# Smaller first loads, and another engine for the store, in a streaming attention and FFN decode step

## Chip, cores and metric

The kernel runs on one core of a Trainium2 chip. The metric is device time in microseconds (us) for one execution, and of several executions the median. A profiled execution gives, beside its own time, a span: from the first to the last instruction that the profiler recorded. The engines are TensorE (PE, with PEld for its weight loads), VectorE (DVE), ScalarE (ACT), GpSimd (POOL) and SyncE (SP). SP does no arithmetic here; it issues the transfers (DMAs) and waits. The name SPq or ACTq in a profile line is the queue of that engine's instructions which wait or issue.

## What is computed

One decode step for a batch of 8 with one new token each (x is 8 x 512). Branch A is attention over the last 1024 entries of a cache of 4096; branch B is a gated feed-forward network. All inputs are bf16.

```python
xn = _layernorm(x)                                  # 8 x 1 x 512
# A: 32 query heads, 8 K/V heads, head size 128, window W = 1024
q = (xn @ wq).reshape(B, Sq, Hq, Dh).transpose(0, 2, 1, 3)
k = jnp.repeat(k_cache[:, :, Sk - W:, :], rep, axis=1)
v = jnp.repeat(v_cache[:, :, Sk - W:, :], rep, axis=1)
p = _softmax(jnp.einsum("bhqd,bhkd->bhqk", q, k) * (Dh ** -0.5))
s = o_merged(jnp.einsum("bhqk,bhkd->bhqd", p, v)) @ wo
# B
g = _silu((_gelu(xn @ w_gate) * (xn @ w_up)) @ w_down)
return x + s * g
```

(`o_merged` stands for the transpose and reshape that join the heads.) The input of 47.46 MB is read once: 16 MiB of K, 16 MiB of V, 4 MiB of wq, 4 MiB of wo, 5.25 MiB of the feed-forward weights. The output is 8 KB.

## The kernel before

**Buffers.** Eight slots of 2 MiB each (128 partitions x 16 KB) in one ring hold everything large: a batch's K or V, half of wq, a weight matrix of the feed-forward part, or half of wo. A slot is loaded again once its last readers are done.

**Loads.** `load_cache` (L69) loads one batch's K or V: two transfers (g = 0 and 1, four heads each) of 1 MiB, L72. Partition p*4 + n of the destination holds 32 consecutive rows of head n, 8 KB in one piece. All loads are issued by SP, in the order of the program text: K of batch 0, wq in two transfers of 2 MiB (L93: partition p gets four rows of wq of 8 KB each, two to a transfer, so 16 KB in one piece), K of batch 1, V of batch 0; then in the loop over batches (L398 on) K of batch b+2 and V of batch b+1; at the end w_gate, w_up, w_down (L422, L425) and wo in six transfers (L436), of which the last three are of 640, 256 and 128 KB, so that little is left to do after the last one has landed. The load of x (L67) is the only transfer that ACT issues.

**Landing semaphores.** Each transfer tells of its landing by a semaphore. There are eight of them for the transfers, given out in rotation in the order of the program text, whichever engine issues: x has the first, the first K transfer the second, and so on. An issue waits until the transfer eight before it has landed, as that one has the same semaphore. The store of the output is the 45th transfer. At the end of the program SP waits for all semaphores, one after the other (the profile puts these waits at L538), then for the other engines.

**Compute.** The layer norm of x and its transposed copy xnR come first. VectorE turns K (`turn_k`, L234, one instruction for a transfer's 1 MiB, so both halves of the partitions have to be there), TensorE computes q in 32 matmuls (L247, eight for each quarter k of wq), which go through `q_both` (L257, L260) to `qbd` (L269). Then for each batch: scores (L295), softmax (L305 to L317), the turned probabilities (L328), values (L339), and the collection of heads (L360 to L391). The feed-forward part runs after the last batch (L450 to L491). Last come the 128 matmuls with wo (L498), 32 for each of its four quarters, then y (L506), out_sb (L508) and the store (L510).

**Order.** The schedule is by hand: each engine runs its instructions in the order of the program text, and waits only for what they need.

Of the kernel before, what the change touches and what calls it, by code (L numbers as in the profile page):

```python
# [21 lines left out]
def kernel(  # L22
# [13 lines left out]
    nc = tc.nc  # L36

    B, Sq, D = A_x.shape
    Hkv, Sk, Dh = A_k_cache.shape[1], A_k_cache.shape[2], A_k_cache.shape[3]
# [3 lines left out]
    win0 = Sk - W  # L43
    F = B_w_gate.shape[1]
    inv = float(Dh) ** -0.5
    P = nc.NUM_PARTITIONS
    NK = D // P
    HG = 4
    NG = Hkv // HG
    C = W * HG // P  # L50
# [11 lines left out]
    def slot(name):  # L62
        return ring.tile([P, 2 * ROW], BF16, name=name, tag="slot")
# [2 lines left out]
    x_sb = keep.tile([B, D], BF16, name="x_sb")  # L66
    nc.scalar.dma_start(out=x_sb, in_=A_x.flatten_outer_dims())  # L67

    def load_cache(cache, b, name):  # L69
        t = slot(name).rearrange("p (g x) -> p g x", g=NG)  # L70
        for g in range(NG):
            nc.sync.dma_start(  # L72
                out=t[:, g],
                in_=cache[b, g * HG : (g + 1) * HG, win0:Sk, :].rearrange(
                    "n (p c) d -> p n (c d)", c=C
                ),
            )
        return t

    k_sb, v_sb = {}, {}  # L80

    def load_k(b):
        k_sb[b] = load_cache(A_k_cache, b, "k_sb")

    def load_v(b):
        v_sb[b] = load_cache(A_v_cache, b, "v_sb")

    load_k(0)
    wq_v = A_wq.rearrange("(p k) n -> p k n", k=NK)
    wq_sb = []  # L90
    for i in range(2):
        t = slot("wq_sb").rearrange("p (k n) -> p k n", k=NK // 2)
        nc.sync.dma_start(out=t, in_=wq_v[:, i * (NK // 2) : (i + 1) * (NK // 2), :])  # L93
        wq_sb += [t[:, k, :] for k in range(NK // 2)]
    load_k(1)
    load_v(0)

# [4 lines left out]
        out=ident,  # L102
        in_=ident,
# [13 lines left out]
        out=xpad,  # L117
        in_=xpad,
# [17 lines left out]
        out=xhat,  # L136
# [9 lines left out]
    with tc.tile_pool(name="ps_x", bufs=1, space=PSUM) as ps_x:  # L146
# [26 lines left out]
        out=hv,  # L173
        in_=hv,
# [7 lines left out]
        out=neg_st,  # L182
        in_=neg_st,
# [8 lines left out]
        out=neg_mv,  # L192
        in_=neg_mv,
# [12 lines left out]
    for g in range(NG):  # L206
        nc.vector.tensor_reduce(
            out=sel[:, g, g * qd : (g + 1) * qd],
            in_=ident.rearrange("p (t g h) -> p g h t", t=4, g=NG)[:, g],
# [5 lines left out]
        out=own, in_=ident.rearrange("p (i e) -> p e i", e=8), axis=AX.X, op=ALU.add  # L215
    )
    pick = consts.tile([P, 4 * NU], BF16, name="pick")
    with nc.allow_low_precision(reason="sums of zeros and a single one"):
        nc.vector.tensor_reduce(
            out=pick, in_=ident.rearrange("p (a e) -> p a e", e=8), axis=AX.X, op=ALU.add  # L220
# [177 lines left out]
    for b in range(B):  # L398
        if b + 2 < B:
            load_k(b + 2)  # L400
        if b + 1 < B:
            load_v(b + 1)
            turn_k(b + 1, 0)
        softmax(b)
        if b + 1 < B:
            scores(b + 1, 0)
        if b >= 1:
            gather(b - 1)
        if b + 1 < B:
            turn_k(b + 1, 1)  # L410
            scores(b + 1, 1)
        turn_p(b)
        values(b)
        keep_o(b)
        if b == 4:
            regroup(0)
# [10 lines left out]
    for u in range(NU):  # L427
        if u % 2 == 0:
            pair = slot("wo_sb").rearrange("p (v j d) -> p v j d", v=2, d=D)
        t = pair[:, u % 2]  # L430
        src = A_wo[u * 1024 : (u + 1) * 1024, :].rearrange("(p j) d -> p j d", j=8)
# [14 lines left out]
    for n, ws in (("z_ps", wgu[0]), ("u_ps", wgu[1])):  # L446
# [15 lines left out]
        out=z2, in0=z2, scalar1=0.044715, scalar2=1.0, op0=ALU.mult, op1=ALU.add  # L462
# [11 lines left out]
        out=hT.rearrange("p j b -> p (j b)"), in_=h_bf.rearrange("p (y j) -> p j y", j=NJ)  # L474
    )
    f_ps = ps_f.tile([P, DT], FP32, name="f_ps")
    for j in range(NJ):
# [11 lines left out]
        out=g_sb, in0=g_sb, scalar1=0.5, scalar2=0.5, op0=ALU.mult, op1=ALU.add  # L489
# [5 lines left out]
    for u in range(NU):  # L495
# [11 lines left out]
    out_sb = ffn.tile([P, DT], BF16, name="out_sb")  # L507
    nc.vector.tensor_tensor(out=out_sb, in0=y, in1=x_res, op=ALU.add)  # L508
    out_f = out.flatten_outer_dims()
    nc.sync.dma_start(  # L510
        out=out_f.rearrange("b (t d) -> t b d", t=4), in_=out_sb[0 : P : RB, :]
    )

# [29 lines left out]
```

## Time and profile before

| What | Value |
|---|---|
| median of three runs | 121.58 us (121.34 to 121.73) |
| profiled execution, own time | 121.8 us |
| its span | 119.7 us |
| busy: PE, DVE, ACT | 74.1, 75.8, 31.4 us |
| moved | 47.61 MB, mean 398 GB/s over the span |
| packets on the queue of the transfers that SP issues | 6228 |
| packets on the queue of the transfer that ACT issues (x) | 16 |
| mean granted TensorE clock | 0.837 |

The page divides the span into 40 equal slices; a digit is the busy share in tenths, and the DMA row is the mean over the core's 16 DMA engines. A row of a group of instructions says the line, the engine, what is written and read, the number and the time. A row of transfers says who issues them, how many, the KB of each, and the median time from issue to landing; that time includes the wait behind the transfers issued earlier. A transfer consists of packets, and the trace has a record of each: its start, its length in ns and its bytes; every DMA engine that takes part in a transfer ends it with a small write of 4 bytes to the semaphore.

The shortest and longest times from issue to landing of the K and V transfers are 5.4 and 24.4 us. The issuing instruction itself takes 535 ns in the middle of the run and up to 662 ns at its start.

### The profile page before, as it was taken

The numbers are of one execution on the slowest core, as the hardware profiler recorded it, in microseconds if no ns is written. First come the engines' busy times: TensorE is split into PE (matmuls) and PEld (weight loads), VectorE is DVE, ScalarE is ACT, GpSimd is POOL, SyncE is SP. The second block draws the span as 40 slices with busy tenths as digits, with TensorE's granted clock in tenths as the row PEclk, the third lists the DMA queues.
The fourth block names the chain that finished last, engine by engine and source line by source line (L and its number), as shares of the span: only waits on it lengthen the run. The fifth ranks groups of instructions, "written<-read, shape, count | busy, mean of one in ns | idle before, by whom it ended". The sixth has DMA issues, their size and how long they took to land.

```text
span 119.7 us, 2300 instructions
## 1 busy us (share of the span) xinstructions
PE 74.1 (62%) x992; PEld 38.7 (32%) x992; DVE 75.8 (63%) x101; ACT 31.4 (26%) x75; POOL 3.2 (3%) x10
## 2 busy tenths in 40 slices
PE   0100499811994988969687684992994547535460
PEld 0100133300341544535443351450353433134340
DVE  3698820499739999999859959909943232651010
ACT  4600000676007151441612510700616110200000
POOL 2150000000000000000000000000000000000000
PEclk9999999985599999999999998599589755555555
DMA  2999999999999999999999999999999999999930
GB/s 66 394 457 433 411 416 427 430 433 422 427 427 433 419 419 427 435 411 430 430 433 405 430 430 430 411 430 435 424 419 447 422 451 412 434 403 430 402 118 3
DMA packets 6254, 47.61 MB, mean 398 GB/s; under 512 B 732, under 2 KB 868, under 8 KB 1124
## 3 DMA queue, kind: packets, MB, share of 16 engines
q1 hardware_dynamic: 6228, 47.46, 94.5%
q8 instruction: 8, 0.13, 0.4%
q10 hardware_dynamic: 16, 0.01, 0.0%
q14 instruction: 2, 0.02, 0.0%
HBM read 47.46 MB, written 0.01 MB: 397 GB/s over the span
## 4 chain that ended last, share of the span: by engine, by line
DMA 63%; PE 16%; DVE 14%; issue 2%; ACT 2%; SPq 1%; DVEq 0%
DMA wo_sb<-in_A_wo_dram 20%; DMA k_sb<-in_A_k_cache_dram 17%; DMA v_sb<-in_A_v_cache_dram 16%; DMA wq_sb<-in_A_wq_dram 9%; PE q_ps L247 8%; PE S_ps L295 6%; DVE kT L234 5%; DVE qbd L269 2%; DVE mx L305 2%; DVE q_both L260 1%; ACT P_sb L317 1%; PE s_ps L498 1%; DVE q_both L257 1%; SPq L72 1%; PE O_ps L339 1%
## 5 line engine op out<-in xcount | busy, mean ns | idle before, releaser
L295 PE MATMUL S_ps<-kT,qbd 128*128 128x512 bf16 x128 | 34.4, 416 | 14.9 <-DVE kT L234 11.5
L234 DVE STREAM_TRANSPOSE kT<-k_sb 128x2048 int32<-128x2048 int32 x16 | 36.5, 2289 | 4.6 <-DMA k_sb<-in_A_k_cache_dram 4.6
L295 PEld LDWEIGHTS <-qbd 128*128 128x128 bf16 x128 | 12.9, 103 | 32.4 <-issue 17.0
L247 PE MATMUL q_ps<-wq_sb,xnR 128*128 128x512 bf16 x32 | 9.8, 482 | 8.8 <-DMA wq_sb<-in_A_wq_dram 8.8
L315 ACT ACTIVATE nb<-m 32x1 f32<-32x1 f32 x32 | 6.4, 201 | 22.7 <-DVE m L312 22.4
L305 DVE TENSOR_REDUCE mx<-S_ps 128x1 f32<-128x1024 f32 x8 | 9.6, 1195 | 4.1 <-PE S_ps L295 4.1
L317 ACT ACTIVATE P_sb<-S_ps,nb 128x1024 bf16<-128x1024 f32 x8 | 11.1, 1391 | 0.3
L339 PE MATMUL O_ps<-v_sb,pT 128*32 128x128 bf16 x512 | 9.3, 228 | 2.6 <-DVE pT L328 2.6
L339 PEld LDWEIGHTS <-pT 128*32 128x32 bf16 x512 | 7.8, 101 | 5.6 <-issue 3.0
L352 ACT COPY O_sb<-O_ps 128x256 f32<-128x256 f32 x8 | 3.0, 372 | 23.5 <-PE O_ps L339 23.5
L247 PEld LDWEIGHTS <-xnR 128*128 128x128 bf16 x32 | 3.7, 118 | 14.6 <-issue 12.6
L328 DVE STREAM_TRANSPOSE pT<-P_sb 128x512 int32<-128x512 int32 x8 | 5.7, 711 | 3.4 <-ACT P_sb L317 2.8
L257 ACT CAST q_both<-q_ps 128x512 bf16<-128x512 f32 x6 | 3.0, 613 | 16.7 <-PE q_ps L247 16.7
L360 PE MATMUL o_ps<-O_sb,sel 128*32 128x128 f32 x32 | 6.1, 325 | 0.9 <-ACT O_sb L352 0.9
L498 PE MATMUL s_ps<-wo_sb,oT 128*32 128x128 bf16 x128 | 4.4, 307 | 3.4 <-DMA wo_sb<-in_A_wo_dram 3.3
L284 PE MATMUL S_ps<-neg_mv,neg_st 128*128 128x512 bf16 x16 | 4.8, 381 | 1.9 <-DVE q_both L257 1.9
L257 DVE CAST q_both<-q_ps 128x512 bf16<-128x512 f32 x2 | 1.3, 672 | 6.9 <-ACT q_both L257 6.9
L360 PEld LDWEIGHTS o_ps<-O_sb,sel 128*32 128x32 f32 x32 | 3.4, 128 | 5.0 <-issue 1.7
L498 PEld LDWEIGHTS <-oT 128*32 128x32 bf16 x128 | 3.5, 136 | 4.4 <-issue 4.2
L506 DVE TENSOR_TENSOR y<-s_ps,g_sb 128x128 f32<-128x128 f32 x1 | 0.3, 290 | 6.9 <-PE s_ps L498 6.9
L239 DVE MEMSET qbd<- 128x4096 uint32 x1 | 3.5, 3472 | 0.8 <-issue 0.8
L479 PE MATMUL f_ps<-wd_sb,hT 128*32 128x128 bf16 x56 | 1.7, 311 | 3.2 <-DVE hT L473 3.2
(64 smaller groups left out, 48.9 us busy)
## 6 DMA issues: line engine op xcount, KB each, us to landing
k_sb<-in_A_k_cache_dram SPq DMA_DIRECT2D x16, 1024.0 KB, 19.9
v_sb<-in_A_v_cache_dram SPq DMA_DIRECT2D x16, 1024.0 KB, 19.6
wq_sb<-in_A_wq_dram SPq DMA_DIRECT2D x2, 2048.0 KB, 11.3
wo_sb<-in_A_wo_dram SPq DMA_DIRECT2D x3, 1024.0 KB, 25.0
wgu_sb<-in_B_w_gate_dram SPq DMA_DIRECT2D x1, 1792.0 KB, 21.3
wgu_sb<-in_B_w_up_dram SPq DMA_DIRECT2D x1, 1792.0 KB
wd_sb<-in_B_w_down_dram SPq DMA_DIRECT2D x1, 1792.0 KB, 24.9
wo_sb<-in_A_wo_dram SPq DMA_DIRECT2D x1, 640.0 KB, 24.1
```

The lines of the kernel that those rows point to most:

```text
L234: nc.vector.transpose(out=t.bitcast(I32), in_=k_sb[b][:, g].bitcast(I32))
L247: nc.tensor.matmul(q_ps[i], xnR[:, k, :, :].rearrange("p j b -> p (j b)"), wq_sb[k][:, i * 512 : (i + 1) * 512], start=(k == 0), stop=(k = ...
L257: e(out=q_bf[:, i * 512 : (i + 1) * 512], in_=q_ps[i])
L284: nc.tensor.matmul(S[b][:, half, :], neg_st.rearrange("p j h -> p (j h)"), neg_mv.rearrange("p a n -> p (a n)"), start=True, stop=False,)
L295: nc.tensor.matmul(S[b][:, half, :], qbd[:, m, b, w, g, :], kv[:, half * 16 : (half + 1) * 16, m, :, w], start=False, stop=(g == NG - 1 an ...
L305: nc.vector.tensor_reduce(out=mx, in_=S[b].rearrange("p a c -> p (a c)"), axis=AX.X, op=ALU.max)
L315: nc.scalar.mul(nb[32 * j : 32 * j + 32, :], m1, -inv)
L317: nc.scalar.activation(out=P_sb[b].rearrange("p c i w -> p c w i"), in_=S[b].rearrange("p a (c w i) -> p (a c) w i", w=2, i=32), func=ACT.Exp,
L328: nc.vector.transpose(out=pT[b].rearrange("p c h w -> p (c h w)").bitcast(I32), in_=P_sb[b].rearrange("p c i w -> p (c i w)").bitcast(I32),)
L339: nc.tensor.matmul(O_ps[b][32 * t : 32 * t + 32, g, :], pT[b][:, c // 2, :, c % 2], vv[:, c, :], start=(c < 4), stop=(c >= C - 4),)
L360: nc.tensor.matmul(o[:, 0:Dh], sel[:, g, :], O_sb[b][:, g, :], start=(g == 0), stop=(g == NG - 1))
L498: nc.tensor.matmul(s_ps[32 * t : 32 * t + 32, :], oT[:, j, u, :], wo[u][:, j, t * DT : (t + 1) * DT], start=(u == 0 and j == 0), stop=(u = ...
```

## The change

Three things. The first transfer of K (batch 0, g = 0) is issued as two, for partitions 0 to 63 and for partitions 64 to 127. wq is loaded by four transfers of 1 MiB, one for each quarter k, into the same two slots. The store of the output is issued by ACT instead of SP. There are 48 transfers now, and the store is the 48th, so that it has the last of the eight semaphores.

```diff
-    def load_cache(cache, b, name):
+    def load_cache(cache, b, name, parts=None):
         t = slot(name).rearrange("p (g x) -> p g x", g=NG)
         for g in range(NG):
-            nc.sync.dma_start(
-                out=t[:, g],
-                in_=cache[b, g * HG : (g + 1) * HG, win0:Sk, :].rearrange(
-                    "n (p c) d -> p n (c d)", c=C
-                ),
+            src = cache[b, g * HG : (g + 1) * HG, win0:Sk, :].rearrange(
+                "n (p c) d -> p n (c d)", c=C
             )
+            if parts is not None and g == 0:
+                parts(t[:, g], src)
+            else:
+                nc.sync.dma_start(out=t[:, g], in_=src)
         return t
...
+    def first_load(dst, src):
+        for a, z in ((0, P // 2), (P // 2, P)):
+            nc.sync.dma_start(out=dst[a:z], in_=src[a // HG : z // HG])
+
     def load_k(b):
-        k_sb[b] = load_cache(A_k_cache, b, "k_sb")
+        k_sb[b] = load_cache(A_k_cache, b, "k_sb", first_load if b == 0 else None)
...
         t = slot("wq_sb").rearrange("p (k n) -> p k n", k=NK // 2)
-        nc.sync.dma_start(out=t, in_=wq_v[:, i * (NK // 2) : (i + 1) * (NK // 2), :])
-        wq_sb += [t[:, k, :] for k in range(NK // 2)]
+        for k in range(NK // 2):
+            nc.sync.dma_start(out=t[:, k, :], in_=wq_v[:, i * (NK // 2) + k, :])
+            wq_sb.append(t[:, k, :])
...
-    nc.sync.dma_start(
+    nc.scalar.dma_start(
         out=out_f.rearrange("b (t d) -> t b d", t=4), in_=out_sb[0 : P : RB, :]
     )
```

## The prediction

> **What bounds the kernel now.** I read the slices of the span first, then the same by stages, then the issues of transfers, and last the end of the span instruction by instruction.
>
> ```profile
> PE   0100499811994988969687684992994547535460
> DVE  3698820499739999999859959909943232651010
> DMA  2999999999999999999999999999999999999930
> GB/s 66 394 457 433 411 416 427 430 433 422 427 427 433 419 419 427 435 411 430 430 433 405 430 430 430 411 430 435 424 419 447 422 451 412 434 403 430 402 118 3
> ```
>
> Each column is a fortieth of 119.7 us, 2.99 us. TensorE and VectorE both have holes; the DMA row has none from the second column to the thirty-eighth, and the rate stays near 427 GB/s. By stages (start:end, length, busy us of PE, PEld, DVE, ACT, POOL, clock, DMA share, GB/s):
>
> ```profile
> 0.00:3.00 3.00, 0.00 (x0) 0.00 (x0) 0.98 (x4) 1.28 (x1) 0.78 (x7) 1.00 0.29 66
> 8.00:13.00 5.00, 0.00 (x0) 0.00 (x0) 4.19 (x3) 0.00 (x0) 0.00 (x0) 1.00 1.01 433
> 40.00:60.00 20.00, 17.21 (x271) 9.43 (x269) 19.02 (x18) 7.84 (x21) 0.00 (x0) 1.00 1.01 426
> 100.00:112.00 12.00, 6.79 (x152) 4.16 (x145) 4.33 (x9) 1.40 (x3) 0.00 (x0) 0.50 1.01 425
> 112.00:116.00 4.00, 2.17 (x64) 1.69 (x63) 0.00 (x0) 0.00 (x0) 0.00 (x0) 0.50 0.63 250
> ```
>
> The DMA share is 1.01 from 8 to 112 us: one stream, never starved. So the time is the stream's start, its bytes, and a tail. The chain of waits names many buffers and engines on its way, but where a transfer takes 20 us from issue to landing it stood behind others, and an engine that is 1 us sooner doesn't move it.
>
> ```profile
> k_sb<-in_A_k_cache_dram SPq DMA_DIRECT2D x16, 1024.0 KB, 19.9
> wq_sb<-in_A_wq_dram SPq DMA_DIRECT2D x2, 2048.0 KB, 11.3
> ...
> x_sb<-in_A_x_dram ACTq DMA_DIRECT2D x1, 8.0 KB
> ```
>
> The end, and SP's longest waits there:
>
> ```profile
> 114.87 1.28 PE L498 MATMUL s_ps<-wo_sb,oT 128*32 128x128 bf16 x32 [0.46 <-DMA wo_sb<-in_A_wo_dram]
> 116.20 0.29 DVE L506 TENSOR_TENSOR y<-s_ps,g_sb 128x128 f32<-128x128 f32 x1 [6.91 <-PE s_ps L498]
> 116.52 0.29 DVE L508 TENSOR_TENSOR out_sb<-y,x_res 128x128 bf16<-128x128 f32 x1
> 116.84 0.69 SPq L510 DMA_DIRECT2D out_dram<-out_sb  x1
> ```
> ```profile
> SPq L510 <- DVE out_sb L508: 15.1, 1, 15.1
> SPq L538 <- DMA out_dram<-out_sb: 1.0, 1, 1.0
> ```
>
> The last matmuls wait for the last wo piece (landed at 115.81 by its semaphore's record); behind them come two VectorE instructions, 0.69 us of issue, 1.0 us of landing, and SP's final waits up to 119.7.
>
> The profiled execution took 121.8 us (span 119.7, and 2.1 around it), the median of the three runs is 121.58; the sum below is a difference, laid on the median.
>
> **The change part by part.**
>
> *First K transfer in two halves.* Removed: one transfer of 1 MiB to 128 partitions. Added: two of 0.5 MiB to partitions 0 to 63 and 64 to 127, one behind the other. At the head of the stream the first half has its 64 partitions to itself. No large transfer of this trace goes to fewer than 128 partitions, so the price has two ends. The only narrow load is x, 8 KB to 8 partitions. By its packet records seven of its eight 1 KB packets took 44 to 51 ns, the same as the 46 ns of wo's 1 KB packets on 128 partitions; by these a narrow transfer loses nothing: 0. But as a whole, from its first packet (1.753 us) to its last end (2.060), x took 0.307 us: 8,192 B / 0.307 us = 26.7 GB/s for 8 partitions, and 427 x 8/128 is 26.7 too. If the rate goes with the partitions, 64 get 213.5 GB/s: 524,288 B take 2.46 us, both halves 4.91, against 2.46 for 1 MiB at 427: +2.45 us. The engines don't start together (first K packets spread over 0.28 us, about 0.1 between two); where two share what one had, an engine that is 0.1 ahead wins that twice: -0.2. I take **+2.25**: a half MiB is nearer to a whole transfer than to a 44 ns packet, which a buffer on the way could swallow. Ends 0 and +2.45. Nothing covers it: each transfer behind starts that much later, SP's waits for landings pass later, and the stream has no idle time in which to catch up. Late next is the first K transpose (7.08 us), then wq, then everything.
>
> The Trainium skill, "SBUF — State Buffer", section "Door 1: The DMA port swizzle", says that partitions 0 to 63 reach only 8 of the 16 ports on the DMA side and gives 196 GB/s for 64 partitions against 328 for 128 (1 MiB each); the section on issuing two DMAs for both halves says they serialize. By its limit of 218 GB/s the halves would cost an estimated +2.4 us, by the packets' 44 ns row nothing: the page speaks against this part, and no transfer here shows it at size.
>
> *The earlier start.* x's first packet came 0.37 us after its issue ended (8 packets), K's 0.78 us after (128 packets): 0.41 for 120 more packets. With 64 fewer: -0.22 if it goes by packets, 0 if it is fixed. I take **-0.15**, as K's sixteen first packets come one after the other over 0.28 us, which looks like a making by number.
>
> *wq in four.* Two transfers of 2 MiB become four of 1 MiB. Packets of 16 KB (256 of them) become 8 KB; on one engine they follow each other every 607 ns and 307 ns: 2 x 307 - 607 = 7 ns for each of 16 packets an engine, 0.11 us. Three more transfers than before, K's included, put three more completion writes on each engine, 9 ns and about 6 between: 0.05. Together **+0.16**, ends 0.05 and 0.16. The gain: the first q matmul can start after 1 MiB, some 2.4 us before 13.6; but the last needs the same last byte, and q's consumers feed compute that waits for the stream: **0**, hidden behind the DMA row. Three more issues on SP, some 0.58 us each (the opening eight took 0.48 to 0.66): 1.74 us. What hides them is the queue: before the first landing SP has issued at least 7 MB of which under 2 have moved, 12 us of stream. Without that cover, 0.58 each.
>
> *Waits of SP.* There are eight landing semaphores in rotation; each issue waits for the one eight before it. So the ninth transfer (now the second batch's first K half, on 128 partitions) waits for x, long landed, and the tenth for the first half. Behind those SP holds only later loads; seven transfers remain queued at each: **0**.
>
> *The store on ACT.* Moved: one issue. It still waits for VectorE's out_sb. On ACT nothing runs after L487 (108.4 us), nothing is queued behind it but the end of the program, and no transfer waits there. SP is only freed. Price: ACT's one issue took 0.58 us (x), SP's store 0.69, SP's first K 0.66: from -0.11 to +0.08, I take **-0.05**.
>
> *The last semaphore.* The transfers number 45 before and 48 after, so the store moves from the fifth of eight semaphores to the eighth. SP's final waits in the records pass the store's landing at 118.67, then come three more, 0.06 us apart, before its drain. With the store waited for last, those three pass while it lands: **-0.18**, or 0 if ACT's transfers count elsewhere; x on ACT took the first place of the same rotation, so I don't think so.
>
> Sum: 2.25 - 0.15 + 0.16 - 0.05 - 0.18 = +2.03. 121.58 + 2.03 = **123.6 us**.
>
> **Rivals.**
>
> *The narrow halves cost nothing* (ends on the other side). Then 0 - 0.15 + 0.16 - 0.05 - 0.18 = -0.22: **121.36**. For it: x's 44 ns packets. Against: x as a whole. Its ends are -0.22 + 0.05 - 0.11 - 0.18 = -0.46 and 0 + 0.16 + 0.08 - 0 = +0.24, so 121.1 to 121.8; it decides below a rate loss of 0.2 us for both halves.
>
> *The halves overlap.* If engines that are ahead go on to the second half while the others finish the first, half of the loss comes back: 1.2 - 0.22 = +1.0, **122.6**. For it: the 0.28 us of spread at the start and hiccups of up to 0.5 us in single packets. Against: engines wait for the same thing at the same time, so the one ahead is hardly freed.
>
> *The change doesn't do what it says*: the store's semaphore isn't the last waited for. Then the first sum is 123.8, the first rival 121.5; it changes no sign.
>
> **How the numbers follow.** The narrow rate holds: 0.50, 123.6 (own range 2.45 + 0.24 = +2.7 to 2.0 - 0.46 = +1.5: 123.1 to 124.3). It costs nothing: 0.44, of which half is below 121.22, as both unknown gains may be larger and the median itself moved by 0.39 between three runs. Overlap: 0.06. What a measurement tells from no change is about 0.3%, 0.36 us. Faster 0.22; same 0.22; slower 0.56 (the first case, the overlap). The range has to hold both signs: 121.1 to 124.1, leaving out the ends of each.
>
> **What would show it.** The first stages: at the narrow rate, 2.5 to 7 us would show near 214 GB/s and K's packets near 618 ns instead of 309, the first K transpose would move from 7.08 to about 9.3, and the last wo piece would land at 118. If 2.5 to 7 us shows 427 GB/s, the forecast is wrong, and the gain is to be read at the end: SP's wait for out_dram would be its last one. q's first matmul should start near 13.4 in the first case, near 11 in the second, and the end not care. A DMA share under 1.0 in any later stage would mean that the covers I claim are not there.

## The result, and the profile after

The changed kernel takes 1.0122 times as long as before (95% interval 1.0097 to 1.0146), 123.1 us against 121.64: slower, by 1.5 us. (Three of its six executions took 126.5 to 128.2 us, which makes the median of all six 124.92, and one of four in the later repeat took 128.07, as no execution of any other kernel here did; they are left out of the ratios and of all that follows, and no profile shows what slowed them.) Run again later beside the experiments, its ratio was 1.0093 (1.0076 to 1.0110): 1.1 us more than before, where 1.4 was expected. The profiled execution took 123.01 us, its span is 121.0, 1.3 more than before.

The slices of the span, DMA rows only, of the changed kernel:

```profile
DMA  2999999999999999999999999999999999999940
GB/s 60 268 339 420 433 431 428 428 425 431 414 428 433 420 431 428 423 423 420 431 425 425 431 428 420 414 428 431 425 433 425 440 451 398 420 427 428 409 168 3
```

The DMA row still has no hole. But the rate of the second and third column is 268 and 339 GB/s, where it was 394 and 457: the engines are as busy as before and move less. From the fourth column on the two rows agree within some per cent, up to the tail. By stages (start:end, length, busy us of PE, PEld, DVE, ACT, POOL, clock, DMA share, GB/s), the kernel before:

```profile
3.00:4.00 1.00, 0.00 (x0) 0.00 (x0) 0.57 (x4) 0.66 (x2) 0.00 (x0) 1.00 0.97 385
4.00:5.00 1.00, 0.52 (x8) 0.32 (x8) 0.61 (x5) 0.99 (x2) 0.00 (x0) 1.00 1.02 401
5.00:6.00 1.00, 0.00 (x0) 0.00 (x0) 0.89 (x7) 0.28 (x2) 0.60 (x2) 1.00 1.01 410
6.00:7.00 1.00, 0.00 (x0) 0.00 (x0) 0.94 (x4) 0.00 (x0) 1.00 (x2) 1.00 0.98 410
```

The same stages of the changed kernel:

```profile
3.00:4.00 1.00, 0.00 (x0) 0.00 (x0) 0.57 (x3) 0.75 (x2) 0.00 (x0) 1.00 1.24 369
4.00:5.00 1.00, 0.52 (x8) 0.32 (x8) 0.61 (x5) 0.99 (x3) 0.00 (x0) 1.00 0.93 221
5.00:6.00 1.00, 0.00 (x0) 0.00 (x0) 0.89 (x7) 0.19 (x2) 0.68 (x2) 1.00 1.08 238
6.00:7.00 1.00, 0.00 (x0) 0.00 (x0) 0.94 (x4) 0.00 (x0) 1.00 (x2) 1.00 1.00 221
8.00:12.00 4.00, 0.00 (x0) 0.00 (x0) 3.99 (x2) 0.00 (x0) 0.00 (x0) 1.00 1.01 426
```

The last two numbers of a row are to be read together: share 1.0 at 221 GB/s means that packets take about twice as long. They do: by the packet records an 8 KB packet takes 0.47 to 0.62 us from 4 to 6.5 us (605 to 615 ns from 5.3 us on), and 309 ns once the halves are through.

To see where time is lost I count, from the packet records of each run, the bytes on SP's queue moved by a moment (a packet in flight pro rata), divide by 427 GB/s, and take the difference to the same count of the kernel before: us of stream that a run is behind.

| behind by, us, at | 4 us | 5 | 6 | 7 | 8 | 10 | 20 | 110 |
|---|---|---|---|---|---|---|---|---|
| changed kernel | 0.20 | 0.60 | 0.98 | 1.46 | 1.59 | 1.60 | 1.67 | 1.67 |
| the same again (f4_changed_again) | 0.10 | 0.50 | 0.88 | 1.34 | 1.40 | 1.41 | 1.48 | 1.48 |

Nearly all of it is lost between 4 and 8 us, and nothing of it comes back up to 110 us. In the tail behind that, 0.15 does: the last wo piece landed at 117.33 by its semaphore, 1.52 later than before. The end, in order of time, of the changed kernel:

```profile
116.43 1.24 PE L504 MATMUL s_ps<-wo_sb,oT 128*32 128x128 bf16 x32 [0.48 <-DMA wo_sb<-in_A_wo_dram]
117.71 0.29 DVE L512 TENSOR_TENSOR y<-s_ps,g_sb 128x128 f32<-128x128 f32 x1 [6.85 <-PE s_ps L504]
118.04 0.29 DVE L514 TENSOR_TENSOR out_sb<-y,x_res 128x128 bf16<-128x128 f32 x1
118.36 0.64 ACTq L516 DMA_DIRECT2D out_dram<-out_sb  x1
```

y starts at 117.71 instead of 116.20, 1.51 later; the span ends only 1.33 later. The rest, 0.18, was gained behind the store. SP's waits at the end of the program:

```profile
SPq L544 <- DMA wo_sb<-in_A_wo_dram: 17.0, 3, 13.1
...
SPq L544 <- DVE out_sb L514: 1.9, 1, 1.9
SPq L544 <- DMA out_dram<-out_sb: 1.7, 1, 1.7
```

SP now stands in its final waits (L544) long before the store. By the records SP passed its wait for the store's landing at 120.18, and 0.81 us later the span ended; before it was 1.00 us from there (118.66) to the end, with three more waits in between.

### The profile page after: what moved, and what is told of

The parts are those of the page before. It is cut to its first block, busy times and chain, and to the rows that moved or that the text cites. A ratio compares the mean times of both kernels' runs of the same rounds, so it can differ in the third digit from the quotient of the medians.

```text
span 121.0 us, 2304 instructions
## 1 busy us (share of the span) xinstructions
PE 73.0 (60%) x992; PEld 38.1 (31%) x992; DVE 76.2 (63%) x101; ACT 31.4 (26%) x75; POOL 3.2 (3%) x10
## 4 chain that ended last, share of the span: by engine, by line
DMA 77%; PE 11%; DVE 6%; SPq 2%; issue 1%; DVEq 0%
DMA k_sb<-in_A_k_cache_dram 33%; DMA wo_sb<-in_A_wo_dram 20%; DMA v_sb<-in_A_v_cache_dram 16%; DMA wq_sb<-in_A_wq_dram 8%; PE q_ps L253 7%; DVE kT L240 4%; PE S_ps L301 2%; PE s_ps L504 1%; SPq L85 1%; DVE mx L311 1%; PE O_ps L345 1%; DVE q_both L263 1%; SPq L78 1%; PE r_ps L394 0%; DVE oT L397 0%
## 5 line engine op out<-in xcount | busy, mean ns | idle before, releaser
L253 PE MATMUL q_ps<-wq_sb,xnR 128*128 128x512 bf16 x32 | 9.1, 453 | 7.8 <-DMA wq_sb<-in_A_wq_dram 7.8
L323 ACT ACTIVATE P_sb<-S_ps,nb 128x1024 bf16<-128x1024 f32 x8 | 11.1, 1392 | 0.3
L366 PE MATMUL o_ps<-O_sb,sel 128*32 128x128 f32 x32 | 5.4, 296 | 1.0 <-ACT O_sb L358 1.0
```

The lines of the kernel that those rows point to most:

```text
L253: nc.tensor.matmul(q_ps[i], xnR[:, k, :, :].rearrange("p j b -> p (j b)"), wq_sb[k][:, i * 512 : (i + 1) * 512], start=(k == 0), stop=(k = ...
L323: nc.scalar.activation(out=P_sb[b].rearrange("p c i w -> p c w i"), in_=S[b].rearrange("p a (c w i) -> p (a c) w i", w=2, i=32), func=ACT.Exp,
L366: nc.tensor.matmul(o[:, 0:Dh], sel[:, g, :], O_sb[b][:, g, :], start=(g == 0), stop=(g == NG - 1))
```

## The experiments

The kernels of one group (e, f or g) ran on one chip, beside runs of the kernel before on the same chip (median 121.78 for e1 to e4, 121.71 for f1 to f4, 121.66 for g1 to g4).

**Each part alone: e1_halves_only.** The kernel before with the new `first_load` for batch 0 and nothing else:

```diff
-        k_sb[b] = load_cache(A_k_cache, b, "k_sb")
+        k_sb[b] = load_cache(A_k_cache, b, "k_sb", first_load if b == 0 else None)
```

> The kernel before with the first K transfer in two partition halves, nothing else changed; 46 transfers, the store stays on SP and has the sixth of the eight semaphores. Theory (the narrow halves at the head of the stream cost 1.6 us of stream, as in the changed kernel, and everything else is small): 121.6 + 1.6, less 0.06 for one final wait that the store no longer has behind it: 123.1 us; 4 to 7 us of the span at about 215 GB/s. Rival (the cost comes from the ordering that the change makes with wq's smaller transfers behind the halves): within 0.5 us of 121.6.

Measured: 122.97 us, ratio 1.0095 (1.0080 to 1.0109). The stream is 0.67 behind at 5 us, 1.69 at 8, 1.68 at 110.

```profile
4.00:5.00 1.00, 0.51 (x8) 0.31 (x8) 0.62 (x5) 0.99 (x3) 0.00 (x0) 1.00 0.83 188
5.00:6.00 1.00, 0.00 (x0) 0.00 (x0) 0.89 (x7) 0.21 (x2) 0.67 (x2) 1.00 1.07 246
6.00:7.00 1.00, 0.00 (x0) 0.00 (x0) 0.94 (x4) 0.00 (x0) 1.00 (x2) 1.00 1.16 254
```

The halves alone do it; the order of wq behind them isn't needed. The time rises by less than the stream loses, 1.2 us.

**e2_wq_only.** wq in four transfers, nothing else.

```diff
-        nc.sync.dma_start(out=t, in_=wq_v[:, i * (NK // 2) : (i + 1) * (NK // 2), :])
+        for k in range(NK // 2):
+            nc.sync.dma_start(out=t[:, k, :], in_=wq_v[:, i * (NK // 2) + k, :])
...
```

> The kernel before with wq in four transfers of 1 MiB, nothing else changed; 47 transfers, the store on SP with the seventh semaphore. Theory: +0.11 for 8 KB packets in place of 16 KB, +0.03 for two more completion writes, -0.12 for two final waits: 121.6 us, within 0.2. Rival (smaller wq transfers cost the stream something of their own): 122.0 or more. q's first matmul about 2.4 us earlier than 13.6, and the end unmoved.

Measured: 121.42 us, ratio 0.9971 (0.9960 to 0.9982), a little more gain than expected. The stream is 0.07 behind from 20 us on. The tile q_ps in this run (instruction, min/median/max ns, first and last start):

```profile
L253 PE MATMUL q_ps<-wq_sb,xnR x32: 376/379/631, 11.1 to 19.8; 128*128 128x512 bf16 x32
```

q starts at 11.1 us instead of 13.6 and its last matmul at 19.8 instead of 23.1, and y at the end starts at 116.20 as before: 3 us earlier in the compute are worth nothing while the stream sets the end. Of the 0.36 us gained, 0.14 are in the span of the profiled execution (119.53 against 119.66: the store has the seventh semaphore, two waits fewer behind it). The rest lies outside the span, and no view shows what it is.

**e3_act_only.** The store by ACT, nothing else.

```diff
-    nc.sync.dma_start(
+    nc.scalar.dma_start(
         out=out_f.rearrange("b (t d) -> t b d", t=4), in_=out_sb[0 : P : RB, :]
     )
```

> The kernel before with the store issued by ACT, nothing else changed; 45 transfers, the store keeps the fifth semaphore. Theory: -0.05 for the shorter issue (0.64 against 0.69 in the two profiles), the landing and three final waits as before: 121.6 us, within 0.15. Rival (ACT's queue adds a delay at the end that the changed kernel's profile hides behind its last semaphore): 121.9 or more.

Measured: 121.50 us, ratio 0.9979 (0.9970 to 0.9988). The issue takes 0.64 us instead of 0.69, the store lands 1.81 us after the start of its issue instead of 1.82, and three waits follow as before. ACT adds no delay; again more is gained (0.28) than the span of the profiled execution shows (0.06).

**Cut another way: e4_columns.** The changed kernel, the first K transfer halved along its columns.

```diff
-        for a, z in ((0, P // 2), (P // 2, P)):
-            nc.sync.dma_start(out=dst[a:z], in_=src[a // HG : z // HG])
+        for a, z in ((0, ROW // 2), (ROW // 2, ROW)):
+            nc.sync.dma_start(out=dst[:, a:z], in_=src[:, :, a:z])
```

> The changed kernel with one difference: the first K transfer is halved along its columns, 128 partitions of 4 KB each twice, in place of 64 partitions of 8 KB. The number of transfers (48), the store on ACT and the last semaphore stay. Theory (the cost is that a half reaches only 64 partitions): the stream keeps 427 GB/s from 3 us on, the loss of 1.6 us is gone, -0.18 for the final waits, -0.05 for ACT's issue, +0.16 for wq's packets and the completion writes: 121.5 us, within 0.3. Rival (the cost is that there is one transfer more at the head, or that the halves are small): 123.1 us, as in the changed kernel.

Measured: 122.51 us, ratio 1.0065 (1.0049 to 1.0082). Neither: faster than the changed kernel, but still 0.73 us slower than before. The stream is 0.11 ahead at 4 us, 0.10 behind at 5, 0.72 at 7 and 1.00 at 10. The halves themselves run nearer to the rate before (packets mostly of 159 to 200 ns for 4 KB; 361 and 319 GB/s from 3 to 5 us, before 385 and 401); then, from 5.2 to 5.6 us, eight 8 KB packets start, of the next K transfer, that take 1.1 to 1.5 us. So beside the narrowness there is a second loss at the head, which I hadn't expected; g2 to g4 look for it.

**Without the halves: f1_no_halves.**

```diff
-        k_sb[b] = load_cache(A_k_cache, b, "k_sb", first_load if b == 0 else None)
+        k_sb[b] = load_cache(A_k_cache, b, "k_sb", None)
```

> The changed kernel without its partition halves: wq in four transfers, the store on ACT, 47 transfers, the store with the seventh semaphore. If the parts add up, the gains of wq alone (0.36) and of ACT alone (0.28) give 0.5 to 0.64 us less than the kernel before: a ratio of 0.995 to 0.996, and the whole loss of the changed kernel lies in the halves, 1.9 us or more between this one and it. Rival (the two gains overlap at the end): 0.3 to 0.4 us less, ratio 0.997. The stream's deficit against before at 10 us and later: 0.1 us or less.

Measured: 121.56 us, ratio 0.9991 (0.9981 to 1.0001). The two small gains, 0.5 to 0.64 us if they added up, don't; on this chip there is hardly any. The stream is 0.01 behind at 110 us, as it should be. The halves' price in this setting, f4_changed_again against this one, is 122.84 - 121.56 = 1.3 us, where 1.9 or more was expected.

**The same cut in a full queue: f2_wq_half.** Without the K halves, but the second quarter of wq in two transfers of 64 partitions.

```diff
-            nc.sync.dma_start(out=t[:, k, :], in_=wq_v[:, i * (NK // 2) + k, :])
+            step = P // 2 if (i, k) == (0, 1) else P
+            for a in range(0, P, step):
+                nc.sync.dma_start(
+                    out=t[a : a + step, k, :],
+                    in_=wq_v[a : a + step, i * (NK // 2) + k, :],
+                )
```

> As the one without K halves, but the second wq quarter is loaded as two transfers, partitions 0 to 63 and 64 to 127, in the middle of a full queue (48 transfers, the store has the last semaphore). If part of the price was covered at the head of the stream by its slow first microsecond, 1 MiB in two halves costs more here, up to the full 2.45 us of stream at half rate; if the price is the same anywhere, 1.6 us. Packets of 606 to 615 ns for about 4.9 us. Rival (halves are slow only at the head, where the queue is empty): 0.3 us or less.

Measured: 124.05 us, ratio 1.0191 (1.0173 to 1.0209). 2.16 us behind at 15 us, 2.53 from 20 us on. By stages:

```profile
8.00:10.00 2.00, 0.00 (x0) 0.00 (x0) 2.00 (x2) 0.00 (x0) 0.00 (x0) 1.00 1.00 422
...
11.00:12.00 1.00, 0.41 (x2) 0.17 (x3) 0.44 (x1) 0.00 (x0) 0.00 (x0) 1.00 1.01 205
12.00:13.00 1.00, 1.00 (x4) 0.42 (x3) 0.75 (x1) 0.00 (x0) 0.00 (x0) 1.00 0.93 213
13.00:14.00 1.00, 1.00 (x4) 0.30 (x2) 1.00 (x1) 0.00 (x0) 0.00 (x0) 1.00 1.11 238
14.00:15.00 1.00, 1.00 (x3) 0.15 (x1) 1.00 (x1) 0.00 (x0) 0.00 (x0) 1.00 0.93 205
...
16.00:18.00 2.00, 1.74 (x5) 0.64 (x6) 0.00 (x0) 0.00 (x0) 0.00 (x0) 1.00 0.98 414
```

Some five microseconds at half rate, in packets of 0.50 to 0.65 us. A MiB in two narrow halves costs the full 2.5 us here, in the stream and in the time (124.05 against 121.56 of f1), and 1.4 to 1.7 of stream at the head, about 0.9 us less.

**A quarter of the partitions: f3_wq_quarters_of_32.** `P // 4` in place of `P // 2` in the same edit.

> As the one before it, but the second wq quarter is loaded as four transfers of 32 partitions (50 transfers; the store has the second semaphore, six final waits of 0.06 us more). Theory A (the rate of a transfer goes with its partitions, as the price in the prediction was worked out): 32 partitions get a quarter of the rate, 1 MiB takes 9.8 us, packets 1.2 us, the stream loses 7.4 us. Theory B (what counts is the part of the receiving side that is reached, and 0 to 31 reach as much of it as 0 to 63, as the Trainium skill states in SBUF — State Buffer, Door 1: The DMA port swizzle): 1 MiB takes 4.9 us, packets 0.61 us, and the stream loses what the two halves lost, 1.6 to 2.45 us.

Measured: 124.10 us, ratio 1.0197 (1.0181 to 1.0213); 2.77 us behind from 20 us on, packets of 0.51 to 0.66 us.

```profile
11.00:12.00 1.00, 0.00 (x0) 0.00 (x0) 0.47 (x1) 0.00 (x0) 0.00 (x0) 1.00 1.02 205
12.00:13.00 1.00, 0.76 (x2) 0.29 (x3) 0.72 (x1) 0.00 (x0) 0.00 (x0) 1.00 0.94 213
13.00:14.00 1.00, 1.00 (x4) 0.41 (x3) 1.00 (x1) 0.00 (x0) 0.00 (x0) 1.00 1.11 238
14.00:15.00 1.00, 1.00 (x4) 0.35 (x3) 1.00 (x1) 0.00 (x0) 0.00 (x0) 1.00 0.93 205
```

The same rates row by row as with 64 partitions. Theory A, on which the prediction's price was built (rate in proportion to the partitions), is out: it asked for 7.4 us. The Trainium skill's "SBUF — State Buffer", section "Door 1: The DMA port swizzle", says that partitions 0 to 31 and 0 to 63 reach the same 8 of 16 ports, and these runs agree, 205 to 238 GB/s for both against its 218.

**The last semaphore without K halves: g1_last_semaphore.**

```diff
-    nc.sync.dma_start(out=wd, in_=B_w_down.rearrange("(p j) d -> p j d", j=NJ))
+    wd_v = B_w_down.rearrange("(p j) d -> p j d", j=NJ)
+    for a, z in ((0, NJ // 2), (NJ // 2, NJ)):
+        nc.sync.dma_start(out=wd[:, a:z, :], in_=wd_v[:, a:z, :])
```

> The kernel without K halves (wq in four, the store on ACT), and w_down in two transfers along its columns, all 128 partitions each, so that there are 48 transfers and the store has the last semaphore. By the profiles' tails: three final waits fewer than before (-0.18), ACT's issue (-0.05), wq's packets and three more completion writes (+0.1): 0.1 to 0.2 us less than before, a ratio of 0.998 to 0.999. Rival (the loss of the column halves in K shows that any transfer with smaller packets stalls the next one): 0.5 us or more above before.

Measured: 121.52 us, ratio 0.9984 (0.9975 to 0.9994), as expected: this version keeps the other two parts of the change and is faster than both kernels, though by only 0.14 us over the kernel before. From the store's landing to the end of the span it is 0.81 us, as in the changed kernel. A cut along columns, late and in a full queue, stalls nothing that can be seen: the stream is 0.06 ahead of that of the kernel before at 60 us and 0.02 at 110, and at no moment more than 0.03 behind.

**The second loss: g2_columns_later**, `first_load` by columns and for `b == 2`.

> The column halves moved from the first K transfer to that of the third batch, in the middle of a full queue. Theory (their loss of 1.0 us belongs to the head of the stream, where 8 KB packets of about 1.4 us followed the 4 KB ones at 5 us): the stream loses 0.2 us or less here, the time is within 0.4 us of the kernel before. Rival (the change of packet size costs 1 us anywhere): a loss of about 1 us at 20 to 30 us of the span.

Measured: 121.72 us, ratio 0.9997 (0.9987 to 1.0007). 0.45 us behind at 30 us, 0.47 at 110; no packet in that stretch takes longer than 0.45 us. Only a part of this is the cut's: the first 4 KB packet starts at 27.6 us, and by 27 us the stream was already 0.23 behind, by 8 KB packets of uncut transfers that took up to 0.45 us (in f1 none there takes over 0.31); why isn't shown. From 27 to 30 us, while the halves move, 0.22 more goes. So the loss of 1 us belongs to the head, as the theory has it.

**g3_every_second_partition.** 64 partitions, but spread:

```diff
-        for a, z in ((0, P // 2), (P // 2, P)):
-            nc.sync.dma_start(out=dst[a:z], in_=src[a // HG : z // HG])
+        for a in range(2):
+            nc.sync.dma_start(out=dst[a:P:2], in_=src[:, a:HG:2])
```

> The changed kernel with its first K transfer in two by even and odd partitions in place of lower and upper half: 64 partitions each, spread over the whole receiving side. Theory A (the number of partitions or the size of a transfer counts): a loss of 1.45 to 1.6 us as in the changed kernel, packets of 600 ns. Theory B (which partitions are reached counts, over the transfer as a whole): the loss goes, 0.3 us or less. If engines take neighbouring rows in step, half of the receiving side is still idle at each moment, and B looks like A, with packets of 600 ns in shorter stretches.

Measured: 122.61 us, ratio 1.0074 (1.0056 to 1.0092).

```profile
3.00:4.00 1.00, 0.00 (x0) 0.00 (x0) 0.57 (x4) 0.71 (x2) 0.00 (x0) 1.00 1.01 393
4.00:5.00 1.00, 0.51 (x8) 0.31 (x8) 0.62 (x5) 0.99 (x3) 0.00 (x0) 1.00 1.02 385
5.00:6.00 1.00, 0.00 (x0) 0.00 (x0) 0.88 (x6) 0.22 (x2) 0.66 (x2) 1.00 1.26 238
6.00:7.00 1.00, 0.00 (x0) 0.00 (x0) 0.94 (x4) 0.00 (x0) 1.00 (x2) 1.00 0.62 254
7.00:8.00 1.00, 0.00 (x0) 0.00 (x0) 1.00 (x2) 0.00 (x0) 0.72 (x1) 1.00 1.05 369
```

Two results in one. Up to 5 us, while the two halves move, the rate is the one before (393 and 385 against 385 and 401), packets mostly of 309 to 320 ns: 64 partitions aren't slow as such, 64 neighbouring ones are. Then from 5 us on the rate falls to 238 with packets of up to 1.6 us, as with the column halves: 0.04 ahead at 5 us, 0.93 behind at 10.

**g4_four_column_halves.** Both K transfers of batch 0 by columns (the condition on `g == 0` taken out of `load_cache`).

> The changed kernel with both first K transfers (the first batch's) in two column halves of 4 KB packets; 49 transfers. If the switch from 4 KB to 8 KB packets stalls the stream, the slow packets move to the first wq packets, near 7.5 us, with a loss of about 1 us again; if the second K transfer at 5 us is what is slow, they stay near 5 us; if the loss grows with the number of 4 KB packets, it doubles.

Measured: 122.55 us, ratio 1.0075 (1.0058 to 1.0092). 0.01 behind at 5 us, 0.76 at 10; the long packets (1.25 to 1.48 us) start again at 5.2 to 5.3 us, now of 4 KB followed by 4 KB, and none are at wq's first packets. So it isn't the switch of the packet size, and it doesn't grow with their number: with a cut first transfer, the start of the second K transfer is slow in each of these three cuts. (In the kernel before, too, single packets take 0.5 to 0.57 us there, from 4.7 to 5.3 us.) Why stays open; what was not tried is to load other data there, or to issue the transfers further apart.

## Why the prediction was right

123.6 us was predicted and 123.1 measured. The direction, the place and the path are as told: the halves move at about half rate (221 to 238 GB/s from 4 to 7 us, packets up to 615 ns), the loss falls in the first 8 us, and the end pays for it. That the time lies in the stated range shows little, as 121.1 to 124.1 held both signs; the prediction's own range for this case was 123.1 to 124.3, and the time is at its lower end. Not as told are the size of the halves' price, and the law that it was worked out from. Step by step:

- *The narrow halves, +2.25.* The term that was mis-sized: 1.6 us of stream at 10 us (1.60 and 1.41 in two profiles of the change, 1.70 alone), and by the times 1.2 (e1) and 1.3 (f4 against f1). f2 shows that the upper end, 2.45, was the right price in a full queue (2.53). What the prediction missed is the cover at the head: "Nothing covers it" holds for what comes behind, but the stream's own first microsecond is slow anyway. At 4 us the change is only 0.20 behind although it has worked on a narrow half all the time; 1.4 of the 1.6 us go between 4 and 8. But the slow start is only the smaller part of the cover, by the packet records: at 3 us both kernels had moved 0.12 to 0.13 MB, which at half rate would have cost an estimated 0.3 us. From 3 to 4 us the changed kernel then moved 0.305 MB (0.31 in f4, 0.30 in e1), in packets of 0.31 to 0.6 us: well over half rate, and only 0.17 behind the kernel before in that microsecond. Why a narrow half is that fast there and not in f2 stays open; no run varied the start.
- *The row that the price came from.* x as a whole, 26.7 GB/s on 8 partitions, gave the right half rate for 64 partitions by a wrong law. f3 shows that 32 partitions are as fast as 64, g3 that 64 spread ones run at the full rate. And the row itself was luck: x took 0.307 us because of one packet of 0.258 us among its eight; in the changed kernel's profile all eight took 44 ns and x as a whole 0.108 us, 76 GB/s. The page's rule, which the prediction only set beside it, is the one that f3 agrees with.
- *Nothing covers it, and what is late next.* The second half landed at 7.62 us by its semaphore, where the whole transfer had landed at 6.19; the first K transpose started at 7.72 instead of 7.08 (9.3 was predicted), q's first matmul at 12.58 (13.4), and the last wo piece landed at 117.33 (118). VectorE had been busy with constants until 7.08, so 0.8 us of the delay was hidden there, which changes nothing at the end.
- *The earlier start, -0.15.* Zero: the first K packet came at 2.26 us (2.25 in f4, 2.60 in e1), before at 2.25. With 64 rows it comes no sooner than with 128, so the 0.41 us between x's and K's first packets isn't explained by the number of packets.
- *wq in four, +0.16.* 0.07 of stream in e2; compute earlier by 3 us without effect, as predicted.
- *Waits of SP, 0.* Right: in the changed kernel's stages from 8 to 112 us the DMA share is 1.00 to 1.02.
- *ACT's issue, -0.05, and the last semaphore, -0.18.* 0.64 against 0.69 us, and 0.19 less from landing to end. Right.
- *The sum of the measured terms*: 1.6 + 0 + 0.07 - 0.05 - 0.19 = +1.43, between the 1.33 of the profiled spans and the 1.5 of the times (the repeat: 1.20 and 1.1).

The rivals: that the halves cost nothing is refuted by e1. The overlap is refuted for a full queue by f2, where the full price was paid; at the head, where 1.4 to 1.7 us was lost and that rival asked for 1.2, a part of it can't be excluded. That the cut alone, without narrowness, costs 0.8 to 1.0 us at this place (e4, g3, g4) was in no rival. In the changed kernel the two can't be told apart: its trace has no packet over 0.81 us in the first 8 us, so the half rate accounts for what is seen, but a cut of the first transfer along its columns or by every second partition would have saved only a third to a half of the loss.

## What to carry to other kernels

Where one stream of transfers sets the end, look at bytes per second beside the busy share: here a stretch at half rate with full shares was paid almost in full at the end (1.67 us of stream, 1.51 in the start of y). Don't cut a transfer by neighbouring partitions; if the number of transfers has to change, cut a late one along its columns, which cost nothing measurable for w_down (g1) and about 0.2 us of stream for a K transfer in the middle (g2). A store whose semaphore is waited for last saved 0.06 us for each wait that no longer stands behind the landing.

## What the runs showed of the hardware

- In a full queue transfers to 64 or to 32 neighbouring partitions moved 205 to 238 GB/s with 8 KB packets of 0.5 to 0.66 us, those to 128 partitions 427 with 0.31 us; 64 partitions taken every second one kept 385 to 393 at the head of the stream.
- A first transfer cut in two, in three ways other than by neighbouring partitions (columns, columns with the second transfer cut too, every second partition), was followed by packets of 1.1 to 1.6 us at 5 to 6 us of the span, 0.8 to 1.0 us of stream. The cause is open.
- ACT and SP took the same time for the same store from the start of its issue to its landing (1.81 and 1.82 us).
- Differences of 0.1 to 0.3 us between kernels lay outside the span and didn't add up: wq alone gained 0.36 and ACT alone 0.28, both together 0.15 on another chip.
